# The last layer's first product by Strassen-Winograd on quarters, with weight sums made by accumulating DMAs

## The chip, the cores and the metric

One core of a Trainium2 chip runs the whole program. The metric is the device time of one execution in microseconds (us), lower is better. Differences under about 0.3% cannot be told from none.

The core has five engines with a queue each, executed in order: PE (matrix products), DVE and ACT (elementwise work; ACT also applies a scale and a bias in one instruction), POOL (elementwise work and DMAs) and SP (here it only issues DMAs). A product accumulates in PSUM, of which the program uses four buffers of two banks. Everything else lies in SBUF (128 partitions) or in device memory (HBM).

## The reference

```python
def _A_ref(x, w_r, w_i):                      # x: 2048 x 640
    return irfft2(rfft2(x) * (w_r + 1j * w_i))

def _B_ref(x, w1, b1, w2, b2):                # mixes along the 2048 rows
    h = _layernorm(x)
    u = gelu(einsum("bsd,sf->bdf", h, w1) + b1)        # F = 1728
    y = einsum("bdf,fs->bds", u, w2) + b2
    return y.transpose(0, 2, 1)

x = x + _A_ref(_layernorm(x), A_w_r, A_w_i)
x = x + _B_ref(_layernorm(x), B_w1, B_b1, B_w2, B_b2)
x = x + _A_ref(_layernorm(x), A_w_r, A_w_i)
x = x + _B_ref(_layernorm(x), B_w1, B_b1, B_w2, B_b2)
```

Both B layers use the same w1 and w2. All of it is float32, and the result must agree to float32 accuracy.

## The kernel before

The four layers run one after the other: A (`a1`, `a2`), B (`b1st`), A (`a1`, `a2`), B (`b2nd`). The change concerns the last one, `b2nd`, and one thing in `b1st`.

To multiply float32 numbers with float16 products, each operand is split in a high and a low float16 part: ACT writes `hi = scale * x`, DVE writes `lo = scale * x - hi`, and `mm3` adds three products, hi times hi, hi times lo and lo times hi. The names `wh`, `wl`, `hh`, `hl`, `u` and `wo` are such parts.

`h`, the normalised input, has 16 row blocks j of 128 x 640, each stored as two halves of 320. `w1` has 14 column tiles of 128 (the last has 64 columns twice, once for the high and once for the low product), `w2` 16 column tiles over 14 row blocks.

First product of `b2nd`: `SEQ` orders the 14 tiles in pairs (t, t + 7). A tile's two raw halves of 128 x 1024 float32 (512 KB) are loaded on SP four tiles ahead (`ahead`, `wload`), split by `wsplit` one tile ahead, and multiplied by 16 blocks of h: 16 x 2 halves x 3 = 96 matmuls, 64 for the last tile. Then come scale, bias and gelu, and `usplit` splits the result u into the parts that the second product needs: with t and t + 7 and the two halves of 320 u is a 2 x 2 matrix of quarters, and the parts are those quarters and their sums T1 to T4.

The second product is already done by Strassen-Winograd: with A a pair of w2 tiles (d, d + 8) cut in quarters A11, A12, A21, A22, and S1 = A21 + A22, S2 = S1 - A11, S3 = A11 - A21, S4 = A12 - S2, seven products of quarters replace eight. For each d `form` makes an S on DVE, `hi` (ACT) and `lo` (DVE) split all seven left operands, `product` runs 7 x 3 = 21 matmuls, and `evict` combines the result into `xt`, the residual with the bias added by `xbias` on ACT. The last u block to be ready, `LATE`, is left out of products 2 and 3 at first and added after them.

The order of work: within one engine the instructions run in program order where `pin` is set, and elsewhere in the order that the framework's scheduler chose at build time. Waits between engines are semaphores; a DMA on SP's or POOL's queue waits in that queue, and what stands behind it waits too. Up to eight DMAs of SP are under way at a time. A product needs a PSUM buffer, which is free once the product four back (with `big`, in turn) has been evicted.

## Time and profile before

| what | value |
|---|---|
| median of three runs | 1030.15 us (1028.54, 1030.15, 1031.58) |
| the profiled execution | 1028.95 us |
| its span, first to last instruction | 1027.2 us |
| mean granted TensorE clock | 0.980 |
| last layer (`b2nd`), first matmul to end | 684.76 to 1027.2 us |
| first product of it | 684.76 to 863.73 us |
| second product of it | 863.73 to 1023.7 us |

The span is that of the profiled execution; 1.75 us of its time lie outside it. In rows that group instructions, "xN" is their number, then follow busy us and mean ns of one, then the idle time of the engine before them and what released it. A timeline row begins with start and duration in us; rows of the chain of waits do so too, and name engine and output.

### The profile page before, as it was taken

What the parts mean: (1) busy time and instruction counts of PE and PEld (TensorE: products, weight loads), DVE (VectorE), ACT (ScalarE), POOL (GpSimd) and SP (SyncE); (2) the same over time, 40 slices, a digit from 0 to 9 for tenths busy, and PEclk for the clock granted to TensorE, in tenths of its full rate; (3) what the DMA queues carried; (4) which work ended last, traced back from release to release, by engine and by line L of the source; (5) the groups of instructions that cost most, each with busy time, mean ns of one, the idle gap of its engine ahead of it and who ended that gap; (6) DMA issues with size and microseconds to landing.
All of it is one profiled execution on the core that took longest, in us unless ns stands there. A gap on an engine that the chain in (4) does not pass through costs nothing.

```text
span 1027.2 us, 20943 instructions
## 1 busy us (share of the span) xinstructions
PE 986.3 (96%) x8379; PEld 735.7 (72%) x8379; DVE 725.5 (71%) x1422; ACT 571.2 (56%) x874; POOL 265.7 (26%) x438
## 2 busy tenths in 40 slices
PE   4889999999999999999998999999999999999998
PEld 3768777677777777777776787776777777777776
DVE  7968978954333956666666797897655564988885
ACT  5847768675554556555542575774544454544541
POOL 6927857500000002222222675780000000000000
PEclk9589999999999999999999999999999999999999
DMA  7855356522222264444312644756322232445511
GB/s 230 277 173 168 116 167 222 207 83 99 77 77 74 72 233 155 138 135 123 124 55 86 214 125 130 223 177 210 108 82 83 72 109 77 141 154 175 164 44 52
DMA packets 55738, 139.48 MB, mean 136 GB/s; under 512 B 6461, under 2 KB 12249, under 8 KB 55641
## 3 DMA queue, kind: packets, MB, share of 16 engines
q1 hardware_dynamic: 54200, 131.97, 40.1%
q0 software_dynamic: 1440, 6.17, 2.0%
q8 instruction: 66, 1.08, 0.4%
q14 instruction: 32, 0.25, 0.1%
HBM read 115.05 MB, written 23.07 MB: 134 GB/s over the span
## 4 chain that ended last, share of the span: by engine, by line
PE 76%; DVE 13%; POOL 3%; issue 3%; DMA 2%; ACT 2%; SPq 0%; POOLq 0%; DVEq 0%; ACTq 0%
PE ps L59 76%; DVE st L59 2%; POOL xt L59 2%; DVE xt L59 2%; DVE f L59 1%; DVE Yl L59 1%; DVE s1l L59 1%; DVE hl L59 1%; DVE ta L59 1%; ACT eh L59 1%; DVE el L59 1%; DMA rest<-s1l 1%; POOL r L59 1%; DVE tb L59 1%; DMA stk<-rest 1%
## 5 line engine op out<-in xcount | busy, mean ns | idle before, releaser
L59 PEld LDWEIGHTS <-wh 128*128 128x128 f16 x2992 | 289.7, 98 | 113.4 <-issue 1.8
L59 PEld LDWEIGHTS <-wl 128*128 128x128 f16 x1616 | 157.9, 98 | 62.2 <-DVE wl L59 0.9
L59 PE MATMUL ps<-hh,wh 128*128 128x320 f16 x896 | 186.6, 299 | 0.7 <-ACT hh L59 0.7
L59 PE MATMUL ps<-hl,wh 128*128 128x320 f16 x896 | 184.7, 299 | 0.0
L59 PE MATMUL ps<-hh,wl 128*128 128x320 f16 x832 | 171.4, 299 | 0.6 <-DVE wl L59 0.6
L59 DVE SCALAR_TENSOR_TENSOR wl<-raw,s,wh 128x1024 f16<-128x1024 f32 (+2 forms) x88 | 105.4, 1202 | 87.4 <-ACT wh L59 87.3
L59 PE MATMUL ps<-uh,wl 128*128 128x320 f16 x448 | 133.1, 299 | 0.0
L59 PE MATMUL ps<-ul,wh 128*128 128x320 f16 x448 | 133.1, 299 | 0.0
L59 ACT ACTIVATE wh<-raw,s 128x1024 f16<-128x1024 f32 (+2 forms) x92 | 94.7, 1047 | 68.4 <-PE ps L59 61.6
L59 PE MATMUL ps<-uh,wh 128*128 128x320 f16 x416 | 124.3, 299 | 0.0
L59 ACT ACTIVATE junk<-raw 128x896 bf16<-128x896 f32 (+1 forms) x60 | 59.6, 994 | 46.5 <-DMA raw<-w 46.4
L59 POOL TENSOR_TENSOR r<-v,mh 128x1 f32<-128x1 f32 x64 | 37.4, 584 | 132.2 <-DVE nm L59 122.6
L59 PE MATMUL ps<-tDi,Yh 128*128 128x322 f16 x320 | 71.3, 300 | 0.2
L59 PE MATMUL ps<-u,wo 128*128 128x320 f16 x504 | 69.9, 299 | 0.0
L59 DVE TENSOR_TENSOR f<-eo 128x256 f32<-128x256 f32 (+1 forms) x124 | 39.1, 368 | 38.8 <-POOL eo L59 38.1
L59 PEld LDWEIGHTS <-wo 128*128 128x128 f16 x504 | 49.3, 98 | 19.1
L59 POOL TENSOR_TENSOR xt<-xt,ec 128x320 f32<-128x320 f32 x64 | 52.4, 841 | 32.8 <-DVE xt L59 32.6
L59 PE MATMUL ps<-ph,tS 128*128 128x321 f16 (+2 forms) x288 | 59.6, 289 | 1.3 <-DVE tb L59 1.3
L59 ACT ACTIVATE z<-xt,nb,r 128x640 f32<-128x640 f32 x31 | 28.5, 919 | 55.8 <-POOL z L59 43.5
L59 DVE BATCH_NORM_STATS2 st<-xt 128x6 f32<-128x320 f32 x126 | 55.3, 481 | 5.7 <-DMA xt<-x 4.6
L59 PE MATMUL ps<-tM,f 128*128 128x128 f32 x160 | 39.5, 426 | 19.8 <-DVE f L59 19.8
L59 POOL TENSOR_TENSOR eo<-z 128x320 f32<-128x320 f32 x62 | 53.3, 880 | 17.1 <-ACT z L59 15.1
(174 smaller groups left out, 1877.0 us busy)
## 6 DMA issues: line engine op xcount, KB each, us to landing
raw<-w SPq DMA_DIRECT2D x56, 512.0 KB
xt<-x SPq DMA_DIRECT2D x79, 320.0 KB
w<-w SPq DMA_DIRECT2D x48, 321.0 KB
x<-xt SPq DMA_DIRECT2D x47, 320.0 KB
raw<-w SPq DMA_DIRECT2D x32, 448.0 KB
raw<-w2z SPq DMA_DIRECT2D x32, 448.0 KB
out<-xt SPq DMA_DIRECT2D x15, 320.0 KB
tIM<-tIM POOLq DMA_DIRECT2D x8, 512.0 KB, 5.6
```

What stands on the lines that cost most here:

```text
L59: i = f(*a, **k)
```

## The change

1. In `b1st`, after a tile's split, `wstore` writes its high and low parts to HBM: those of w1 (`wst`, on POOL's queue) and those of w2 (`wst2`, on SP's). Of the tiles t and t + 7 (or d + 8) it keeps A11, A12 and A22; A21 is never multiplied alone. Tiles 6 and 13 of w1 are not stored.
2. In `b2nd`, tiles 6 and 13 of w1 are multiplied as before (96 + 64 matmuls). The other twelve form six pairs (d, d + 7), d = 0 to 5, and each pair takes seven products of quarters of 8 x 3 = 24 matmuls, 168 in place of 192. A11, A12 and A22 are read back split (`fetch`, on SP, four products ahead). S1 to S4 are made in SBUF by DMAs on POOL's queue that add to what is there (`more`, `accum_op=ADD`): a base is loaded on SP (`begin`), and each `more` adds a quarter of w1 from HBM. Signs are moved to the other operand and the eviction, so only sums are needed: S1 = A21 + A22, S2 = S1 + A11, S4 = S2 + A12 and S3 = A11 + A21. For pair 0 each S has its own buffer and its adds are issued at the start of the layer; for the others S1, S2 and S4 are one buffer in turn, and the next add is issued after the low part of the one before. `hi` and `lo` are now for S only.
3. The right operands are sums of quarters of h, made in place on DVE (`tsum`, 128 x 4 x 320 each) and split by `thi` (ACT) and `tlo` (DVE). The parts of h are made four blocks at a time (`hlow`).
4. Each product is evicted by itself (`evict`: A11 twice on ACT, S1 twice on ACT, S2 and S3 two steps on DVE, and so on). The order of products interleaves pairs 0 to 2 and 4, 5 (`first`, `end`).
5. In the second product A11, A12 and A22 come from `wst2` (with a `memset` on POOL of the half of the last row block that is padding), S1 to S4 are formed and split as before. The raw parts of w2 (`load2`), not loaded ahead during the first product, are issued after the fetches for its first six products. The pairs 0 and 1 are interleaved, and the first four products leave `LATE` out at first.

```diff
-SEQ = [t + 7 * i for t in (0, 6, 1, 2, 3, 4, 5) for i in range(2)]
+SEQ = [6, 13]
...
+        self.wst = {
+            t: self.dram.tile([128, 2, 2, 8, 128] if t < 6 else [128, 2, 8, 128], F16, name=f"wst{t}")
+            for t in range(NFT - 1) if t != 6
+        }
+        self.wst2 = {
+            t: self.dram.tile([128, 2, 2, 7, 128] if t < NQ else [128, 2, 7, 128], F16, name=f"wstb{t}") for t in range(NJ)
+        }
...
+        k, t, n = self.wtile(m)
+        st, whole, eng = (self.wst2, NQ, self.nc.sync) if k else (self.wst, 6, self.nc.gpsimd)
+        if t not in st:
+            return
+        for i, w in enumerate(self.w[m]):
+            q = w[:, :n].rearrange("p (c b) f -> p c b f", c=2)
+            eng.dma_start(*((st[t][:, :, i], q) if t < whole else (st[t][:, i], q[:, 1])))
...
                 self.wsplit(m + 1, (c,))
+                if c:
+                    self.wstore(m + 1)
...
+        for j in range(8, NJ):
+            T.activation(hhb[:, j - 8], hf[j], AF.Copy)
...
+        PB = {"A11": "B11", "S1": "T1", "S2": "T2", "A12": "B21", "S3": "T3", "S4": "B22", "A22": "T4"}
...
+        first = "A11.0 A12.0 A11.1 A12.1 S1.0 S2.0 S3.0 S4.0 A22.0 S1.1 S1.2 A11.2 S2.1 S3.1 A22.1 S4.1 A12.2 S2.2 S3.2 A22.2 S4.2"
+        end = "S1.4 A11.4 A12.4 S2.4 S3.4 S1.5 A22.4 S4.4 A11.5 S2.5 A12.5 S3.5 S4.5 A22.5"
+        one = first.split() + each([3], "S1 A11 A12 S2 S3 A22 S4") + end.split()
+        two = "A11.0 A11.1 A12.0 A12.1 A22.0 A22.1 S1.0 S2.0 S3.0 S4.0 S1.1 S2.1 S3.1 S4.1".split()
+        two += each(range(2, NQ), "A11 S1 S2 S3 A12 S4 A22")
+        N1, NP = len(one), len(one) + len(two)
+        ops = [(int(q[-1]), q[:-2], PB[q[:-2]]) for q in one + two]
+        at = {ops[n][:2]: n for n in range(N1)}
...
+        places = [(px, "wo0"), (px, "wo1"), (self.wp[0], "wl"), (self.wp[1], "wl"), (self.wp[0], "wh"), (self.wp[1], "wh")]
...
+        def begin(d, a):
+            pool, tag = (self.wr[1], "Sa") if a == "S1" else (self.wr[0], "raw")
+            cur[d, a] = raw(pool, tag, 2, 8)
+            nc.sync.dma_start(cur[d, a], w1(d, "A21" if a == "S1" else "A11"))
+
+        def more(d, a, b):
+            G.dma_start(cur[d, a], w1(d, b), accum_op=ADD)
...
+        def fetch(n):
+            if n >= NP or ops[n][1][0] == "S":
+                return
+            f, (d, a, _) = int(n < N1), ops[n]
+            st, m = (self.wst, d) if f else (self.wst2, d)
+            w = place(n, 8 if f else 7)
+            nc.sync.dma_start(w, st[m][:, int(a[2]) - 1] if a[1] == "1" else st[m + (7 if f else NQ)])
+            if not f and a[2] == "2":
+                G.memset(w[64:, :, 6], 0.0)
...
+            if n < N1:
+                src[n] = cur[d, a] if (d, a) in cur else cur[d, "S1"]
+            w = place(n, 8 if n < N1 else 7)
+            T.activation(w[:, 0], src[n], AF.Identity, scale=scale(n))
...
+            V.scalar_tensor_tensor(w[:, 1], src[n], scale(n), w[:, 0], op0=MUL, op1=SUB)
+            if d and n < N1 and a in ("S1", "S2"):
+                more(d, "S1", "A11" if a == "S1" else "A12")
...
+        def tsum(a, c, W=V):
+            j, k = slice(4 * c, 4 * c + 4), slice(8 + 4 * c, 12 + 4 * c)
+            B11, B12, B21, B22 = hfa[:, j, 0], hfa[:, j, 1], hfa[:, k, 0], hfa[:, k, 1]
+            o, x, y = {"T1": (B12, B12, B11), "T2": (B22, B22, B12), "T3": (B11, B22, B11), "T4": (B21, B21, B22)}[a]
+            W.tensor_tensor(o, x, y, op=SUB)
...
+        def thi(a):
...
+                T.activation(TT[a][0][:, 4 * c:4 * c + 4], tsrc(a, c), AF.Copy)
...
+            for c in range(2):
+                j = slice(4 * c, 4 * c + 4)
+                V.tensor_tensor(TT[a][1][:, j], tsrc(a, c), TT[a][0][:, j], op=SUB)
...
+        def hlow(c):
+            j = slice(4 * c % 8, 4 * c % 8 + 4)
+            if c < 2:
...
+            else:
+                V.tensor_tensor(hlb[:, j], hfa[:, 4 * c:4 * c + 4], hhb[:, j], op=SUB)
...
+            if a == "A11":
+                ms[d] = self.t(p, [128, 320], F32, "m", 2)
+                act(ms[d])
+                act(f[:, 0], bias=b0)
+            if a == "A12":
+                add(f[:, 0], f[:, 0])
+            if a == "S1":
+                act(f[:, 1], k=self.c1n[:, d:d + 1], bias=b0)
+                act(f[:, 3], bias=b1)
+            if a == "S2":
+                vs[d] = self.t(p, [128, 320], F32, "v", 1)
+                add(vs[d], ms[d], SUB)
+                V.tensor_tensor(f[:, 1], f[:, 1], vs[d], op=SUB)
+            if a == "S3":
+                add(vs[d], vs[d], SUB)
+                T.activation(f[:, 2], vs[d], AF.Identity, scale=-1.0, bias=b1)
+                V.tensor_tensor(f[:, 3], f[:, 3], vs[d], op=SUB)
+            if a == "S4":
+                add(f[:, 1], f[:, 1])
+            if a == "A22":
+                add(f[:, 2], f[:, 2])
...
+        for d in range(1, ND):
+            n, k = at[d, "S1"], at[d, "S3"]
+            stage[max(n - 9, 0)].append(lam(begin, d, "S1"))
+            stage[max(n - 8, 0)].append(lam(more, d, "S1", "A22"))
+            stage[max(k - 11, 0)].append(lam(begin, d, "S3"))
+            stage[max(k - 10, 0)].append(lam(more, d, "S3", "A21"))
...
+        fetch(0)
+        fetch(1)
+        begin(0, "S1")
+        more(0, "S1", "A22")
+        self.wsplit(1, hi=False)
+        begin(0, "S3")
+        pr = self.push("br", side=self.sp)
+        for a in ("S2", "S4"):
+            cur[0, a] = pr.tile([128, 8, 128], F32, name=f"{a}r{self.n}")
+            nc.sync.dma_start(cur[0, a], w1(0, "A21"))
+        for a, q in (("S2", "A22"), ("S4", "A22"), ("S2", "A11"), ("S3", "A21"), ("S4", "A11"), ("S4", "A12")):
+            more(0, a, q)
+        for e in stage[0]:
+            e()
...
+        early, late, low, high = range(NJ - 4), range(NJ - 4, NJ), range(8), range(8, NJ)
+        for js in (early, late):
+            prod(pss[0], wh0, hhigh, js, start=True)
+            prod(pss[0], wl0, hhigh, js)
+            prod(pss[1], wh1, hhigh, js, start=True)
+        fetch(2)
+        fetch(3)
+        hlow(0)
+        hlow(1)
+        for i, w in enumerate((wh0, wh1)):
+            prod(pss[i], w, hlows, low)
+        product(0)
+        hlow(2)
+        hlow(3)
+        for i, w in enumerate((wh0, wh1)):
+            prod(pss[i], w, hlows, high, stop=True)
+        for a in ("T1", "T2"):
+            for c in range(2):
+                tsum(a, c)
+        thi("T1")
+        hi(4)
+        thi("T2")
+        tlo("T1")
+        lo(4)
+        hi(5)
+        tlo("T2")
...
+        T.activation(f[:, A2], pv, AF.Identity, scale=cc, bias=bb)
+        pv, sw = pss[1][:, :, :320], f[:, A4]
+        T.activation(sw[:64], pv[64:], AF.Copy)
+        T.activation(sw[64:], pv[:64], AF.Copy)
+        V.tensor_tensor(sw, pv, sw, op=ADD)
...
+        lo(5)
+        thi("T3")
+        hi(6)
+        tlo("T3")
+        lo(6)
+        last[2] += [lam(tsum, "T4", 0), lam(tsum, "T4", 1), lam(thi, "T4")]
+        last[3] += [lam(tlo, "T4")]
+        last[6] += [dup1, g0(0), g1(0), g0(1), g0(2), g1(1), g1(2), g0(3)]
...
+        for n in range(1, N1):
+            product(n)
+            for e in first[n]:
+                e()
+            if n == 1:
+                hi(7)
+            if n == 2:
+                lo(7)
+            if n > 4:
+                hi(n + 3)
+                lo(n + 3)
+            for e in last[n]:
+                e()
+            for e in stage[n]:
+                e()
+            fetch(n + 4)
...
+        evict(D5, "A22")
...
+        left = {d: 7 for d in range(NQ)}
+        for (d, a), n in at2.items():
+            if a[0] == "S":
+                n -= N1
+                todo[n - 4 - (d > 1 and a == "S1")].append(lam(form, N1 + n, p))
+        for d in range(2):
+            for a in ("A21", "A22", "A11", "A12"):
+                load2(d, a)
+            xload(d)
+        xload(2)
         xbias(0)
-        FORM = {3: 5, 5: 4, 6: 4, 1: 4}
-        for n in range(NP + 1):
...
+        xbias(1)
+        rest = [j for j in range(7) if j != LATE]
+        for n in range(NP2 + 1):
+            if n < NP2:
+                d, a, _ = ops[N1 + n]
+                if n > 3 or n % 2 == 0:
+                    big = self.big()
+                bank[n] = big[:, n % 2 if n < 4 else 0, :320]
+                product(n, rest if n < 4 else rest + [LATE], stop=n > 3)
             if n == 3:
-                for k in (2, 3):
-                    product(k, [LATE])
-            for k in {0: (), 3: (), 4: (2, 3)}.get(n, (n - 1,)):
+                for k in range(4):
+                    product(k, [LATE], start=False)
+            for k in {0: (), 1: (), 2: (), 3: (), 4: (0, 1, 2, 3)}.get(n, (n - 1,)):
                 evict(k)
...
+            if n == 5:
+                xbias(2)
+            if n > 2:
+                hi(N1 + n + 3)
+            if n > 3:
+                lo(N1 + n + 2)
+            for e in todo[n]:
+                e()
+            fetch(N1 + n + 4)
+            for e in extra[n]:
+                e()
+            if n < NP2 and a == "S4" and d + 2 < NQ:
+                for b in ("A21", "A22", "A11", "A12"):
+                    load2(d + 2, b)
```

How instructions move, at the two places of which the prediction speaks. First the start of the last layer on ACT; `hf` is h in float32, `T1h` the high part of T1, `wh <- Sa` and `wh <- S2r` the high parts of S1.0 and S2.0 (pair 0), `fr` tiles 6 and 13, `m` and `f` the eviction of A11.0, `wo <- raw` and `wo <- S4r` the high parts of S3.0 and S4.0. Before, the splits of the next tiles of w1 stood there:

```order
L59 ACTIVATE hh_1371_10059<-hf_1202_9237 128x640
L59 ACTIVATE hh_1371_10061<-hf_1202_9238 128x640
L59 ACTIVATE wl_10366<-raw_10129,s_72 128x8x64
L59 ACTIVATE f_10303<-ps_10141,b1s,c_74 128x640
L59 ACTIVATE q_10305<-ps_10141,b1s,c_74 128x640
L59 ACTIVATE wh_10311<-raw_10125,s_72 128x1024
```

Now:

```order
L59 ACTIVATE T1h_10117<-hf_9285 128x1280 x2
L59 ACTIVATE wh_10362<-Sa_10137,sp_79 128x1024
L59 ACTIVATE T2h_10119<-hf_9285 128x1280 x2
L59 ACTIVATE wh_10369<-S2r_10147,sp_79 128x1024
L59 ACTIVATE fr_10377<-ps_10159,b1s,c_74 128x640
L59 ACTIVATE fr_10377<-ps_10160 64x640 x2
L59 ACTIVATE T3h_10121<-hf_9285 128x1280 x2
L59 ACTIVATE wo_1391_10387<-raw_10142,sp_79 128x1024
L59 ACTIVATE m_10418<-ps_10297,c_74 128x320
L59 ACTIVATE f_10417<-ps_10297,b1s,c_74 128x320
L59 ACTIVATE wo_1395_10421<-S4r_10149,sp_79 128x1024
L59 ACTIVATE T4h_10123<-hf_9285 128x1280 x2
```

Between the end of h and the first eviction of a product there are now four operand sums' high parts and three of S. On DVE, which feeds them, stands at the same place now:

```order
L59 TENSOR_TENSOR hf_9285<-hf_9285 128x4x320 x4
L59 TENSOR_TENSOR T1l_10118<-hf_9285,T1h_10117 128x1280 x2
L59 SCALAR_TENSOR_TENSOR wh_10362<-Sa_10137,sp_79,wh_10362 128x1024
L59 TENSOR_TENSOR T2l_10120<-hf_9285,T2h_10119 128x1280 x2
L59 TENSOR_TENSOR fr_10377<-ps_10160,fr_10377 128x640
L59 TENSOR_TENSOR hf_9285<-hf_9285 128x4x320 x2
L59 SCALAR_TENSOR_TENSOR wh_10369<-S2r_10147,sp_79,wh_10369 128x1024
L59 TENSOR_TENSOR T3l_10122<-hf_9285,T3h_10121 128x1280 x2
L59 SCALAR_TENSOR_TENSOR wo_1391_10387<-raw_10142,sp_79,wo_1391_10387 128x1024
L59 SCALAR_TENSOR_TENSOR f_10417<-ps_10392,c_74,f_10417 128x320
L59 SCALAR_TENSOR_TENSOR wo_1395_10421<-S4r_10149,sp_79,wo_1395_10421 128x1024
L59 TENSOR_TENSOR hf_9285<-hf_9285 128x4x320 x2
```

The rows `hf <- hf` are the sums T1 and T2 (four rows), T3 and T4 (two each), and the last `f` row is the eviction of A12.0.

The second place is the boundary of the two products on SP. Before, the raw parts of w2 came in among those of w1, four tiles ahead, and the `xt` of the residual after them:

```order
L834 DMA raw_11177<-w 128x1024
L834 DMA raw_11179<-w 128x1024
L834 DMA raw_11295<-w2z 128x896
L834 DMA raw_11297<-w2z 128x896
L834 DMA raw_11417<-w2z 128x896
L834 DMA raw_11419<-w2z 128x896
```

Now (`wstb` are the stored parts of w2; the second of these rows is A22.1's fetch, into the place of the first product's last operand):

```order
L1201 DMA wh_11872<-wstb_102 128x1792
L1201 DMA wh_11893<-wstb_103 128x1792
L1404 DMA raw_11824<-w2z 128x896
L1404 DMA raw_11826<-w2z 128x896
L1404 DMA raw_11828<-w2z 128x896
L1404 DMA raw_11830<-w2z 128x896
L1559 DMA xt_11832<-x_0_146 128x640
L1559 DMA xt_11832<-x_8_154 128x640
L1404 DMA raw_11835<-w2z 128x896
L1404 DMA raw_11837<-w2z 128x896
L1404 DMA raw_11839<-w2z 128x896
L1404 DMA raw_11841<-w2z 128x896
```

The second pair's two `xt` rows follow. On ACT there stands now, after the last high part of u:

```order
L59 ACTIVATE u_1427_10804<-q_11756,su 128x320
L59 ACTIVATE xt_11832<-xt_11832,b2s 128x640 x2
L59 ACTIVATE xt_11843<-xt_11843,b2s 128x640 x2
L59 ACTIVATE wo_1531_11947<-S_1530_11915,sp 128x896
L59 ACTIVATE m_1534_11973<-ps_11853,c_75 128x320
L59 ACTIVATE m_1535_11976<-ps_11853,c_75 128x320
L59 ACTIVATE wo_1536_11981<-S_1532_11949,sp 128x896
```

The bias rows of the pairs 0 and 1 stand ahead of the first high part of an S (S1.0), and the evictions `m` of A11.0 and A11.1 behind it.

More of the change, by code (lines that the diff above doesn't have):

```diff
@@ L1139, in b2nd @@
-        px = self.push("px", side=self.sp)
-        pu = self.push("u", side=self.sp)
-        u = [pu.tile([128, 2, 7, 320], F16, name=f"u{f}_{self.n}") for f in range(7)]
-        p = self.push("b1", side=self.sq)
-        for m in (2, 3, 4, 5):
-            self.wload(m)
-        def ahead(m):
-            self.wload(m + 4)
-            if m + 1 < NFT:
-                self.wopen(m + 1)
-        PQ = ("A11", "B11"), ("S1", "T1"), ("S2", "T2"), ("S3", "T3"), ("A12", "B21"), ("S4", "B22"), ("A22", "T4")
@@ L1166, in form @@
+        def form(n, p=None):
             if n >= NP:
@@ new lines, in b2nd, with product, gelu @@
+        bank = {}
+        def product(n):
+            d, a, b = ops[n]
+            o = bank[d, a] = self.big()[:, 0, :320]
+            w = wo[n]
+            for j in range(8):
+                self.mm3(o, (w[:, 0, j], w[:, 1, j]), operand(b, j), j == 0, j == 7)
+        gc, gs = 1.0 / GC, GS * GC
+        fs, qs = {}, {}
+        def gelu(k, x, q, s=slice(None)):
+            x, q = x[:, s], q[:, s]
+            if k == 0:
+                T.activation(q, x, AF.Square)
+            if k == 1:
+                V.scalar_tensor_tensor(q, q, gc, x, op0=ADD, op1=MUL)
+            if k == 2:
+                T.activation(q, q, AF.Tanh, scale=gs)
+            if k == 3:
+                V.scalar_tensor_tensor(x, q, 1.0, x, op0=ADD, op1=MUL)
@@ new lines, in b2nd, with half, go, split1 @@
+        u = {t0: self.u6}
+        for k in range(3):
+            last[9 + k].append(lambda k=k: usplit(k, t0, f))
+        last[12] = [uopen] + last[12]
+        D5 = ND - 1
+        q5 = {}
+        def half(i, *ks):
+            def go():
+                if i // 2 not in q5:
+                    q5[i // 2] = self.t(p, [128, 2, 320], F32, "q", 2)
+                for k in ks:
+                    gelu(k, fs[D5][:, i:i + 1], q5[i // 2][:, i % 2:i % 2 + 1])
+            return go
+        def split1(i, n, x):
+            return [lambda: uhi(D5, i, n, fs[D5][:, x:x + n]), lambda: ulo(D5, i, n, fs[D5][:, x:x + n])]
```

360 lines of the change are left out of this document (183 added, 177 removed).

## The prediction

> **What bounds the kernel now.** I read the page first, then the chain of waits, then windows and the timeline of the last layer.
>
> ```profile
> span 1027.2 us, 20943 instructions
> PE 986.3 (96%) x8379; PEld 735.7 (72%) x8379; DVE 725.5 (71%) x1422; ACT 571.2 (56%) x874; POOL 265.7 (26%) x438
> 703.39 3.96 DMA raw<-w
> 712.13 311.52 PE ps L59 x2292
> ```
>
> PE is busy for 96% of the span, and the last link but one of the chain is 311.52 us of matmuls with nothing between them. Whatever takes matmuls out of that stretch shortens the kernel, as long as nothing makes PE wait instead. The stretches of the last layer (start, first product, second product: columns are us, then busy us of PE, PEld, DVE, ACT, POOL, then clock, DMA share, GB/s):
>
> ```profile
> 684.75:700.00 15.25, 14.90 (x109) 10.41 (x108) 14.54 (x27) 7.62 (x12) 7.40 (x10) 1.00 0.35 115
> 700.00:863.70 163.70, 163.09 (x1201) 117.21 (x1200) 92.68 (x117) 79.19 (x97) 0.00 (x0) 1.00 0.34 107
> 863.70:1023.50 159.80, 159.80 (x1178) 114.92 (x1175) 131.28 (x162) 72.01 (x85) 0.00 (x0) 1.00 0.38 121
> ```
>
> In the first product DVE is at 57% and ACT at 48%; both can take more. The timeline gives the edges and the price of a matmul:
>
> ```profile
> 684.76 2.35 PE L59 MATMUL ps<-hh,wh 128*128 128x320 f16 x16
> 695.34 0.43 PE L59 MATMUL ps<-hh,wh 128*128 128x320 f16 x2 [0.19 <-ACT hh L59]
> 697.78 2.47 PE L59 MATMUL ps<-hh,wl 128*128 128x320 f16 x17
> 863.73 8.31 PE L59 MATMUL ps<-u,wo 128*128 128x320 f16 x60
> 1017.77 3.02 PE L59 MATMUL ps<-u,wh 128*128 128x320 f16 x21
> 1020.62 3.02 PE L59 MATMUL ps<-u,wl 128*128 128x320 f16 x21
> 1023.68 0.55 DVE xt L59
> ```
>
> From 1017.77 to 1020.62 are 21 matmuls: 2.85 us, 0.1357 us each. The first product (13 tiles of 96 and one of 64, 1312 matmuls) runs from 684.76 to 863.73, 178.97 us, which is 1312 x 0.1357 and 0.9 of waiting.
>
> **The gain.** The first product becomes 96 + 64 matmuls (tiles 6 and 13) and 6 pairs x 7 products x 24 = 1008: 1168, so 144 fewer. The second product keeps 56 x 21. 144 x 0.1357 = 19.5 us if PE never waits more than now. The end after 1023.68 is unchanged.
>
> **Work that hides.** In layer 1 about 9.4 MB of w1 parts and 11 MB of w2 parts are stored in some 180 and 215 us, about 52 GB/s each.
>
> ```profile
> 215.00:265.00 50.00, 50.00 (x374) 36.04 (x373) 21.47 (x52) 29.72 (x44) 0.00 (x0) 1.00 0.29 98
> 365.00:415.00 50.00, 50.00 (x392) 36.50 (x391) 28.79 (x79) 29.55 (x43) 8.68 (x21) 1.00 0.58 193
> 35.00:40.00 5.00, 4.54 (x19) 3.91 (x18) 4.96 (x14) 4.82 (x13) 4.57 (x10) 0.50 0.98 345
> ```
>
> There PE is busy throughout with the DMA engines at 0.29 to 0.58, and they have moved 345 GB/s when full, so the stores cost nothing; without that cover each 50 us would have 2.6 MB more, 7.5 us. In the steady part of the first product a pair takes 168 x 0.1357 = 22.8 us of PE. Its work for DVE and ACT comes from these rows:
>
> ```profile
> L59 DVE SCALAR_TENSOR_TENSOR wl<-raw,s,wh 128x1024 f16<-128x1024 f32 x24 | 30.7, 1284 | 44.4 <-ACT wh L59 44.4
> L59 ACT ACTIVATE wh<-raw,s 128x1024 f16<-128x1024 f32 x22 | 25.2, 1144 | 40.3 <-PE ps L59 35.0 <-issue 5.2
> L59 DVE SCALAR_TENSOR_TENSOR xt<-ps,cp,xt 128x320 f32<-128x320 f32 x32 | 17.6, 551 | 20.7 <-ACT m L59 11.7 <-PE ps L59 8.9
> L59 ACT ACTIVATE m<-ps,cp 128x320 f32<-128x320 f32 x8 | 4.2, 522 | 11.6 <-PE ps L59 11.6
> L59 DVE TENSOR_TENSOR fs<-f,fs 128x320 f32<-128x320 f32 x14 | 6.8, 489 | 0.2
> L59 DVE SCALAR_TENSOR_TENSOR u<-fs,su,u 128x960 f16<-128x960 f32 x6 | 7.3, 1218 | 1.8 <-ACT u L59 1.8
> L59 ACT ACTIVATE u<-fs,su 128x960 f16<-128x960 f32 x6 | 6.6, 1096 | 4.0 <-DVE fs L59 4.0
> L59 DVE TENSOR_TENSOR hl<-hf,hh 128x640 f16<-128x640 f32 x16 | 11.8, 820 | 0.0
> L59 ACT ACTIVATE hh<-hf 128x640 f16<-128x640 f32 x2 | 1.3, 722 | 0.0
> L59 DVE SCALAR_TENSOR_TENSOR u<-f,su,u 128x640 f16<-128x640 f32 x7 | 6.2, 880 | 0.0
> L59 ACT ACTIVATE u<-f,su 128x640 f16<-128x640 f32 x7 | 5.8, 827 | 8.2 <-DVE f L59 8.2
> ```
>
> DVE: four low parts of S (5.1), five evictions from PSUM (2.8), six sums of 320 (2.9), four gelu steps of 640 at the 0.82 of hl (3.3) and splits of u of 320, 640 and 1280 (3.0): 17 us, 75%. ACT: four high parts (4.6), six evictions of 320 (3.1), four gelu steps at the 0.72 of hh (2.9) and u's high parts (2.8): 13 us, 59%. Both fit, at shares that DVE has in the second product now (131.28 of 159.80) without a wait of PE. In the second product three splits of seven leave DVE and ACT; per 20 us three fetches of 0.459 MB come in addition, so the traffic rises from about 158 to 227 GB/s (4.5 MB in 20 us; the row is further down), under 345. I cost both at 0.
>
> **The start, +5.0 us.** Here the chain over DVE and ACT is longer than PE's work. Clocks, from the timeline:
>
> ```profile
> 689.83 2.47 DVE L59 SCALAR_TENSOR_TENSOR wl<-raw,s,wh 128x1024 f16<-128x1024 f32 x2
> 692.21 8.17 DVE L59 TENSOR_TENSOR hl<-hf,hh 128x640 f16<-128x640 f32 x11
> 691.61 1.48 POOL L59 TENSOR_SCALAR nb<-mv,r 128x1 f32<-128x1 f32 x1
> L59 DVE SCALAR_TENSOR_TENSOR wh<-raw,s,wl 128x512 f16<-128x512 f32 x2 | 1.5, 752 | 0.0
> L59 ACT ACTIVATE sw<-ps 64x640 f32<-64x640 f32 x2 | 1.4, 698 | 2.0 <-PE ps L59 2.0
> L59 DVE TENSOR_TENSOR sw<-ps,sw 128x640 f32<-128x640 f32 x1 | 0.8, 825 | 2.9 <-ACT sw L59 2.9
> ```
>
> No operation of 1280 is in the trace. On DVE 640 to 960 adds 1.056 ns an element (an estimate from u's rows, 880 and 1218), so 820 + 640 x 1.056 = 1.50, and 1.42 back to back (8.17 / 11 = 0.743 against 820). On ACT, by u's 827 and 1096 and hh's 722, likewise 1.26. DVE: tile 13's halves end at 691.3, the four low parts of h at 697.0, the two of 2560 at 702.6, the sums T1 and T2 at 708.2, T1's low parts at 711.1, low S1.0 at 712.3, T2's at 715.2, tile 13's fold at 716.0, sums T3 at 718.8, low S2.0 at 720.1, T3's at 722.9, low S3.0 at 724.2, A12.0's eviction at 724.7. ACT follows DVE: T3's high parts end at 720.1, high S3.0 at 721.2, and only then A11.0 is evicted, 722.3. PE: 96 high matmuls to 697.8 as now, 32 low to 702.1, A11.0 to 705.4, 32 to 709.7, A12.0 713.0, A11.1 716.4, A12.1 719.6. S1.0 needs A11.0's buffer: 722.3, a wait of 2.7; S2.0 runs to 728.8. S3.0 needs A11.1's, whose eviction stands on ACT behind high S4.0 and T4's high parts, which wait for T4's sums (728.8): 731.1, a wait of 2.3. After it DVE has caught up. Bounds: 2 (operations as short as their overlapped time everywhere) and 9 (0.15 us more for each of some 25 hand-overs).
>
> **The accumulating DMAs, 0 in the sum.** None is in the trace. The nearest rows are POOL's plain loads of the same size:
>
> ```profile
> L59 POOL DMA_DIRECT2D tIM<-tIM x6: 573/625/629, 131.9 to 660.8; - x6
> DMA to landing us min/median/max: 4.2/5.6/7.5
> ```
>
> POOL is free at 693.1. S2.0 needs two in a row and S4.0 three: by 7.5 each 708.1 and 715.6, while ACT reaches them at about 712 and 722. In a pair S1 to S2 to S4 has three products, 9.8 us, for a landing and a split (2.4), so up to 7.4 costs nothing, and PE feels it only some 3 us later. Per pair five plain transfers and four sums of 0.524 MB (128 x 1024 x 4 bytes): 13.7 us of full engines if a sum costs as much as a copy. With a factor k the time is (2.62 + 2.10 k) / 0.345, which passes 22.8 at k = 2.5. I take the row, so 0, and keep k up to 2.75 for the range.
>
> **Between the products, +7.0 us.** SP issues in order. Its last fetch ahead (A22.1 of w2) waits for the last matmul of the first product, t0; behind it stand four raw parts of w2, two xt, four raw, two xt. ACT adds the bias to both xt pairs before the high part of S1.0, and m1 of the first two products comes after that. Until the second xt pair: 9 x 0.459 + 4 x 0.328 = 5.44 MB, at 345 GB/s 15.8 us, and 2.4 us for landing (3.96 for a raw of 0.524 MB, in the chain, less 1.5): t0 + 18.2.
>
> ```profile
> L59 ACT ACTIVATE xt<-xt,b2s 128x640 f32<-128x640 f32 x16 | 12.3, 813 | 0.0
> L59 ACT ACTIVATE wo<-S,sp 128x896 f16<-128x896 f32 x16 | 16.7, 1041 | 39.2 <-DVE S L59 39.2
> L59 DVE SCALAR_TENSOR_TENSOR wo<-S,sp,wo 128x896 f16<-128x896 f32 x16 | 18.3, 1145 | 0.0
> 960.00:980.00 20.00, 20.00 (x149) 14.39 (x148) 16.79 (x21) 8.93 (x10) 0.00 (x0) 1.00 0.51 158
> ```
>
> Bias 0.8, high part 1.04 (20.0), m1, eviction, m1, eviction 2.15 (22.2), two evictions and the low part 2.25: t0 + 24.4. PE reaches S1.0 after six products, 126 x 0.1357 = 17.1, and its third matmul needs the low part: a wait of 7.0. The next products then come at DVE's pace, about 2.85 each, so nothing is won back. Before, these loads stand ahead of time. The ends are 4.6 (no landing time) and 8.3 (the 121 / 0.38 = 318 GB/s of the second product's row). [...]
>
> **The sum.** The profiled run was 1028.95 (span 1027.2 and 1.75 around it): 1028.95 - 19.5 + 5.0 + 7.0 = 1021.4. The three runs shown have median 1030.15, 1.2 above the profiled one; I take half of that: **1022**.
>
> **Rivals.** *Nearly the whole gain, 1010 to 1014*: ACT's bias waits and the start's buffers come free earlier than walked. For it: now PE waits 0.19 there and DVE is seldom the last. Against: the order of ACT and SP leaves no other way. 19.5 less 4 or so: 1028.95 - 15.5 = 1013. *The sums in DMA become the bound, 1031 to 1050*: from k = 2.5 each of five pairs waits. At k = 3 a pair takes 25.9, +3.1 x 5 = 15, and the seven sums of the start with 2.6 MB of plain loads (13.6 MB, 39 us) end at 732 where ACT wants 722: +10. 1021 + 25 = 1046. For it: 27 sums on one queue beside the fetches. Against: the engines have room for a factor of two. [...] *The gain is used up, 1027 to 1033*: DVE does not catch up after the start, and each later pair loses 1 us more to its order of waits: 1021.4 + 6 = 1027.
>
> **How the numbers follow.** Forecast (1014 to 1027) 0.47, nearly whole gain 0.18, sums in DMA 0.22, used up 0.13. Leaving out a third of the second and the part of the third above k = 2.75 (1036), the range is 1010 to 1036; the forecast's own is 1014 to 1027. A measurement here tells 0.3%, 3.1 us, from no change: faster (under 1027) 0.65, same 0.11, slower 0.24.
>
> **What would show it.** In the changed profile: 144 matmuls fewer; PE waiting on ACT f or m about 720 and 729, some 5 us together; ACT idle on DMA xt after the first product and PE waiting some 7 us there; no wait for ACT wh or wo behind DMA Sa in the steady pairs. Landing times of Sa over 8 us, or PE waits at every pair, would speak for the second rival. A PE busy through the boundary would break my largest loss.

## The result: 1036.5 us, slower by 0.6%

| kernel | median us | runs | ratio to before |
|---|---|---|---|
| before | 1030.24 | 6 | 1 |
| changed | 1036.48 (1033.50 to 1039.52) | 6 | 1.0064 [1.0040, 1.0087] |

The prediction was 1022, faster. The profiled run of the changed kernel took 1039.52, 3.0 above the median of its six, with a span of 1037.7. From its page: the span, PE's busy time and count, the chain by line, and POOL's DMA queue (packets, MB, share of the 16 engines' span).

```profile
span 1037.7 us, 20977 instructions
PE 974.2 (94%) x8235; PEld 724.2 (70%) x8235; DVE 737.6 (71%) x1446; ACT 560.4 (54%) x872; POOL 308.7 (30%) x505
q0 software_dynamic: 8016, 29.77, 12.0%
PE ps L59 68%; DMA S4r<-w 3%; DMA xt<-x 2%; POOL xt L59 2%; DVE st L59 2%; DVE f L59 2%; DVE Yl L59 1%; DVE xt L59 1%; DVE s1l L59 1%; DVE hl L59 1%; DVE ta L59 1%; ACT eh L59 1%; DMA raw<-w2z 1%; POOL eo L59 1%; POOL r L59 1%
```

The 144 matmuls are gone (8379 to 8235), and PE is busy 12.1 us less (not 19.5: part of its work ran at a lower clock, below), yet the span is 10.5 longer: PE waits instead. A DMA of `S4r`, a sum of the first pair, now stands in the chain. The timeline of PE before the last layer's products gives a mark that divides the loss: the last matmul of the second A layer's inverse transform (`tIM`). The first A layer has such a matmul too. Both, in the changed kernel, and then in the kernel before:

```profile
188.02 0.31 PE L59 MATMUL ps<-eh,tIM 128*128 128x322 f32 x1
...
696.72 0.31 PE L59 MATMUL ps<-eh,tIM 128*128 128x322 f32 x1
```

```profile
186.54 0.30 PE L59 MATMUL ps<-eh,tIM 128*128 128x322 f32 x1
...
684.61 0.31 PE L59 MATMUL ps<-eh,tIM 128*128 128x322 f32 x1
```

Up to this mark 12.1 us are lost, in a part of the program where little more was changed than that stores were added and `h` became one tile. Of them 1.5 are there already at the first layer's row, ahead of every store; over all profiles of this document that row lies between 184.8 and 188.0, in no order that an edit would give. So profiles are compared below from that row to the mark: 498.1 us before, 508.7 in the changed kernel, 10.6 more. From the mark to the end the old kernel takes 342.6 and the new 341.0, so of the 19.5 only 1.6 remain. Where the other 17.9 went, PE's waits from 680 on say (in total, times, longest):

```profile
PE ps L59 <- ACT f L59: 7.1, 2, 5.4
PE ps L59 <- DVE xt L59: 3.9, 1, 3.9
PE ps L59 <- ACT fr L59: 1.8, 1, 1.8
PE ps L59 <- DVE wo L59: 1.3, 1, 1.3
```

That is 8.9 at the start (`f`, `fr`) and 5.2 between the products (`xt`, `wo`). The waits of 5.4 and of 3.9 end at 747.5 and 887.6. Windows of 2 us behind them (columns as in the windows before; the clock stands third from the end):

```profile
746.00:748.00 2.00, 0.47 (x2) 0.26 (x2) 2.00 (x3) 2.00 (x5) 0.00 (x0) 0.79 1.05 281
748.00:750.00 2.00, 2.00 (x9) 1.19 (x8) 1.90 (x5) 2.00 (x3) 0.00 (x0) 0.50 0.52 156
750.00:752.00 2.00, 2.00 (x15) 1.32 (x14) 1.85 (x3) 1.74 (x4) 0.86 (x1) 0.86 0.00 0
...
890.00:892.00 2.00, 2.00 (x10) 1.12 (x8) 2.00 (x4) 1.04 (x1) 0.00 (x0) 0.50 0.28 41
892.00:894.00 2.00, 2.00 (x9) 1.14 (x8) 2.00 (x4) 0.85 (x1) 0.00 (x0) 0.52 0.91 349
```

The granted clock is halved for some 3 us behind the first gap and some 6 behind the second, which the wait of 1.3 (`wo`) interrupts. By PE's timeline the 24 matmuls of S3.0, the product behind the first gap, take 4.73 us from start to start (747.53 to 752.26) where 24 x 0.1357 = 3.26 would do: 1.5 lost. Behind the second, 40 take 7.57 (889.56 to 897.13) where 5.43 would do: 2.1. Waits of 14.1 and clock of 3.6, less the 0.9 of waits that the old kernel has behind its mark, make 16.8 of the 17.9; 1.1 is not attributed.

For the loss ahead of the mark, SP's timeline in layer 1's second product (start, us, queue, line):

```profile
353.63 8.92 SPq L853 DMA_DIRECT2D raw<-w  x3
363.51 0.60 SPq L891 DMA_DIRECT2D wstb<-wh  x1
364.78 0.51 SPq L891 DMA_DIRECT2D wstb<-wl  x1
365.34 0.84 SPq L853 DMA_DIRECT2D raw<-w  x1
```

The load of a `raw` part (w2, line 853) now comes right behind a pair of stores (`wstb`, line 891), which wait for the finished parts. SP takes them in order, so a load leaves only when the tile before it has been split and stored. Window 380 to 400 shows the price, first before, then changed:

```profile
380.00:400.00 20.00, 20.00 (x159) 14.64 (x158) 9.84 (x33) 11.35 (x16) 4.61 (x11) 1.00 0.67 235
```

```profile
380.00:400.00 20.00, 15.51 (x110) 10.77 (x110) 8.33 (x24) 9.21 (x13) 3.54 (x9) 0.98 0.89 313
```

PE is no longer full, and the DMA engines are at 0.89 and 313 GB/s where the prediction had seen room.

### The profile page after: what moved, and what is told of

It is laid out like the page before. It is cut to its first block, busy times and chain, and to the rows that moved or that the text cites. A ratio compares the mean times of both kernels' runs of the same rounds, so it can differ in the third digit from the quotient of the medians.

```text
span 1037.7 us, 20977 instructions
## 1 busy us (share of the span) xinstructions
PE 974.2 (94%) x8235; PEld 724.2 (70%) x8235; DVE 737.6 (71%) x1446; ACT 560.4 (54%) x872; POOL 308.7 (30%) x505
## 4 chain that ended last, share of the span: by engine, by line
PE 68%; DVE 13%; DMA 6%; POOL 4%; ACT 4%; issue 3%; SPq 0%; POOLq 0%; DVEq 0%; ACTq 0%
PE ps L59 68%; DMA S4r<-w 3%; DMA xt<-x 2%; POOL xt L59 2%; DVE st L59 2%; DVE f L59 2%; DVE Yl L59 1%; DVE xt L59 1%; DVE s1l L59 1%; DVE hl L59 1%; DVE ta L59 1%; ACT eh L59 1%; DMA raw<-w2z 1%; POOL eo L59 1%; POOL r L59 1%
## 5 line engine op out<-in xcount | busy, mean ns | idle before, releaser
L59 PEld LDWEIGHTS <-wh 128*128 128x128 f16 x2602 | 252.0, 98 | 105.3 <-issue 6.7
L59 PEld LDWEIGHTS <-wo 128*128 128x128 f16 x756 | 75.4, 100 | 42.3 <-issue 7.7
L59 PE MATMUL ps<-hl,wh 128*128 128x320 f16 x504 | 104.1, 299 | 0.0
L59 DVE SCALAR_TENSOR_TENSOR wl<-raw,s,wh 128x896 f16<-128x896 f32 (+2 forms) x64 | 74.6, 1170 | 25.1 <-ACT wh L59 25.1
L59 ACT ACTIVATE wh<-raw,s 128x896 f16<-128x896 f32 (+2 forms) x68 | 67.3, 1011 | 10.7 <-PE ps L59 9.1
L59 PE MATMUL ps<-u,wo 128*128 128x320 f16 x420 | 61.4, 306 | 5.2 <-DVE xt L59 3.9
L59 PE MATMUL ps<-hha,wh 128*128 128x320 f16 x304 | 61.5, 299 | 1.1 <-ACT wh L59 1.1
L59 PE MATMUL ps<-tM,f 128*128 128x128 f32 x160 | 37.6, 402 | 22.5 <-DMA xt<-x 12.4
L59 PE MATMUL ps<-tDi,Yl 128*128 128x322 f16 x192 | 55.7, 299 | 1.7 <-DVE Yl L59 1.7
```

Of the source, the lines that this page charges most:

```text
L59: i = f(*a, **k)
```

## The experiments

Times are medians, and the runs of before beside them had medians of 1029.35 (first four kernels), 1029.81 (next four) and 1028.80 (last four); ratios are to these.

**1. The stores, put into the kernel before.** `before_stores` is the kernel before with `wstore` and its calls; `before_w1stores` keeps only w1's, which POOL issues.

```diff
+        self.wstore(0)
+        self.wstore(1)
...
+                if c:
+                    self.wstore(m + 1)
```

> The kernel before plus the change's stores of the split w1 and w2 parts in layer 1, which nobody reads. In the changed kernel's profile the last layer starts 12 us later than before. If the stores cost that (theory 1: SP's queue stands still behind the w2 stores; theory 2: their traffic), 1039 to 1042 us against 1030.2. If the shift comes from the other edits (theory 3), 1030 to 1032.

> The kernel before plus only the w1 stores, on POOL's queue. Theory 1 (waiting stores in SP's queue): 1030 to 1032. Theory 2 (traffic, 9.4 of the 20.4 MB): 1034 to 1037. Theory 3: 1030 to 1031.

Measured: 1036.90, ratio 1.0069 [1.0050, 1.0089], and 1029.82, 1.0008 [0.9997, 1.0019]. The stores of w1 cost nothing that can be told; those of w2 on SP cost 7. PE's waits in layer 1 of `before_stores` that are not in the kernel before:

```profile
PE ps L59 <- DVE sqb L59: 3.5, 1, 3.5
PE ps L59 <- DVE ul L59: 1.5, 1, 1.5
```

`sqb` is the scale's sum over a raw part: the load was late.

**2. The changed kernel without most stores, and with later ones.** `after_nostores` stores tile 0 alone and fetches it in place of every other (the A parts of both products are then others than the reference's). `after_late` keeps all, but issues a w2 tile's stores on SP one tile later, behind the next `raw` load.

```diff
-                if c:
+                if c and m + 1 < NFT:
                     self.wstore(m + 1)
+                elif c:
+                    held.append((m + 1, self.w[m + 1]))
```

> The changed kernel with the stores of tile 0 alone (4 in place of 56); every fetch of the last layer reads that tile, so the first and second product use wrong A parts, with the same bytes moved there. Theories 1 and 2: the 12 us at the start of the last layer go, 1024 to 1027 us. Theory 3: 1035 to 1037.

> The changed kernel with each w2 store issued one tile later on SP, behind the next loads, when its split is long done. Theory 1 (the queue stands still): 1026 to 1031. Theory 2 (traffic): 1035 to 1038, unchanged.

Measured: 1032.21, 1.0025 [1.0010, 1.0040], and 1033.75, 1.0036 [1.0019, 1.0053]. In the changed kernel the stores cost some 4 us (1.0064 to 1.0025); issued later they cost about 1, which the intervals do not tell from nothing. Single runs of `after_late` lie between 1028.9 and 1036.0, and its profiled one, 1030.02, is the second fastest of ten; why they spread so was not found. From the first layer's row to the mark `after_nostores` takes 502.2 us and `after_late` 501.9, so the stall is gone in both, but even without stores it is 4.1 more than before. `after_late` moves the same bytes as the changed kernel, so the stall is one of the queue and not of the traffic; the medians point the same way, but their intervals overlap. ACT's timeline at the start of layer 1's products in `after_nostores` shows one cause:

```profile
209.14 1.06 ACT L59 ACTIVATE junk<-raw 128x1024 bf16<-128x1024 f32 x1 [10.58 <-DMA raw<-w]
```

The scan of a raw w1 part waits 10.58 us for its load. Its buffer reuses the memory of `h`, and since `h` is one tile, the load waits for the last reader of all of it. Experiment 7 undoes this.

**3. SP's order between the products.** `late_xt` is `after_late` with the first two `xt` pairs ahead of most raw parts of w2.

```diff
-        for d in range(2):
-            for a in ("A21", "A22", "A11", "A12"):
-                load2(d, a)
-            xload(d)
+        load2(0, "A21")
+        load2(0, "A22")
+        xload(0)
+        xload(1)
+        load2(0, "A11")
+        load2(0, "A12")
+        for a in ("A21", "A22", "A11", "A12"):
+            load2(1, a)
         xload(2)
```

> The changed kernel with late w2 stores, and at the boundary of the two products SP issues two raw parts, both xt pairs, then the other raw parts. If the wait there is for the second xt pair, as the prediction says, the 4.8 us of waits and some 3 us of half clock after them go: 1025 to 1028 against 1033.8 without it. If the next thing (raw parts, DVE) takes its place: 1031 to 1034.

Measured: 1026.25, 0.9961 [0.9945, 0.9977], 0.75% or 7.7 us better than its base and faster than before. The windows at the boundary, first `after_late`, then `late_xt`:

```profile
860.00:880.00 20.00, 15.17 (x110) 10.45 (x109) 10.54 (x18) 10.53 (x16) 0.31 (x1) 0.95 0.77 302
880.00:900.00 20.00, 20.00 (x132) 13.66 (x131) 19.90 (x25) 7.30 (x7) 0.00 (x0) 0.88 0.69 226
```

```profile
860.00:880.00 20.00, 18.39 (x134) 12.79 (x133) 15.08 (x24) 12.20 (x19) 0.31 (x1) 1.00 0.84 321
880.00:900.00 20.00, 20.00 (x149) 14.26 (x148) 19.86 (x26) 7.29 (x7) 0.00 (x0) 1.00 0.73 235
```

In 40 us 283 matmuls start where 242 did: 41 x 0.1357 = 5.6 us, part of it by the clock, which stays at 1.00. The two profiled runs differ by 5.9 us behind the mark (340.3 and 334.4).

**4. ACT's order at the start.** `late_evict` is `after_late` with A11.0 evicted before T3's high parts and A11.1 before T4's.

```diff
         V.tensor_tensor(sw, pv, sw, op=ADD)
+        evict(0, "A11")
...
+            if n == 2:
+                evict(1, "A11")
             for e in last[n]:
                 e()
```

> The changed kernel with late w2 stores, and ACT evicts A11.0 before T3's high parts and A11.1 before T4's. Theory A (the prediction's: the chain over DVE and ACT makes the waits at the start): they fall from 8.3 to about 2, 1027 to 1030. Theory B (S4.0's accumulating DMAs make them): 1033 to 1035.

Measured: 1033.41, 1.0030 [1.0015, 1.0045], no different from its base. ACT's timeline:

```profile
730.08 1.15 ACT L59 ACTIVATE wo<-S4r,sp 128x1024 f16<-128x1024 f32 x1 [4.84 <-issue]
```

ACT stands still 4.84 us before the high part of S4.0, whose sum has not landed, and the eviction of A11.1 is queued behind it. Of PE's two waits for `f`, 6.8 us in the base, one is gone; the other, 4.4, stays behind the late sum. What the order gains there is lost further on: in the 40 us from 100 us after the mark PE's windows count 282 matmuls, 300 in the base, and PE now waits for low parts of S (`wh` 0.6, `wl` 0.4).

**5. The first pair's sums on POOL instead of in the DMAs.** `late_pool` loads the four quarters of pair 0 plainly and makes S1.0 to S4.0 with five additions on POOL.

```diff
+        for a, b in (("A22", "A21"), ("A21", "A11"), ("A12", "A11"), ("A11", "A22"), ("A12", "A22")):
+            G.tensor_tensor(raw0[a], raw0[a], raw0[b], op=ADD)
```

> The changed kernel with late w2 stores, and the four sums of pair 0 made by five additions on POOL from four plain loads, in place of seven accumulating DMAs on four loads. Theory A: 1032 to 1034, the start's waits stay near 5. Theory B: the start's waits fall to about 5 or less and the clock stays up, 1026 to 1030.

Measured: 1038.55, 1.0083 [1.0067, 1.0100], the slowest of all; from the mark to the end the profile has 347.3 us for the 340.3 of its base. DVE is slower while POOL adds, 10.01 and 9.87 us for two groups that take 5.69 and 5.55 on DVE in `late_xt`, where POOL adds nothing. POOL's timeline, then DVE's:

```profile
702.54 3.48 POOL L59 TENSOR_TENSOR Sa<-Sa,raw 128x1024 f32<-128x1024 f32 x1
714.43 4.93 POOL L59 TENSOR_TENSOR A12r<-A12r,A22r 128x1024 f32<-128x1024 f32 x1
```

```profile
697.36 10.01 DVE L59 TENSOR_TENSOR hl<-hf,hha 128x1280 f16<-128x1280 f32 x4
707.29 9.87 DVE L59 TENSOR_TENSOR hlb<-hf,hhb 128x2560 f16<-128x2560 f32 x2
```

Once POOL is done (719.36) DVE is back at its pace: of T1's two sums (717.08 to 722.12) the first lets ACT start at 720.75, so the second takes some 1.4 us, as in `late_xt`, where T1's and T2's four take 5.69. What POOL's additions would take by themselves no run shows.

**6. All three together, and `h` in separate tiles in layer 1.** `late_all` joins 3, 4 and 5 and splits `hf` again where the layer is the first.

```diff
+        if first:
+            self.hf = [ph.tile([128, 2, 320], F32, name=f"hf{j}_{self.n}") for j in range(NJ)]
+        else:
+            self.hfa = ph.tile([128, NJ, 2, 320], F32, name=f"hf{self.n}")
```

> All three of these at once, and in layer 1 the normalised input in 16 tiles as before (in the changed kernel it is one tile, and the raw loads that reuse its place wait for its last reader). If the waits are separate: 1012 to 1019. If taking one away brings up another: 1024 to 1031.

Measured: 1030.62, 1.0009 [0.9996, 1.0022]: what the order and the tiles give is about what the additions on POOL cost by themselves in experiment 5 (4.8 us above their base).

**7. Separate tiles alone.** `xt_sep` is `late_xt` with the edit of 6.

> late_xt with h of the first layer in sixteen separate tiles again (the last layer keeps its one tile). Theory: in one tile the raw loads that reuse its memory wait for the last reader of all of it, which costs layer 1 about 2 us: last tIM matmul about 686.5 instead of 688.5, time 1024 (0.994 to 0.995 of before). Rival (that wait is hidden behind PE's other work): last tIM matmul within 0.5 of late_xt's, time 1026.

Measured: 1023.61, 0.9947 [0.9932, 0.9961], 0.14% better than `late_xt`, which is less than can be told, and the intervals overlap. The mark is at 687.8 for 688.5, but the first layer ended 1.6 later in this profile; from its row to the mark it is 500.3 us for 502.6, 2.3 less, where about 2 were expected. The scan that waits 10.58 us above and 9.01 in `late_xt` has short waits here, the longest:

```profile
201.40 1.06 ACT L59 ACTIVATE junk<-raw 128x1024 bf16<-128x1024 f32 x1 [2.17 <-DMA raw<-w]
```

The wait is shown to come from the one tile; its price, 1.4 us by the medians and 2.3 by the profiles, is at the edge of what these runs tell.

**8. Plain copies in place of the sums.** `xt_copy` is `late_xt` with `accum_op` left out, so the S matrices of the first product are single quarters of w1.

```diff
-            G.dma_start(cur[d, a], w1(d, b), accum_op=ADD)
+            G.dma_start(cur[d, a], w1(d, b))
```

> late_xt with every accumulating DMA turned into a plain copy of the same bytes on the same queue; the matrices S1 to S4 of the first product are then single quarters of w1, so its products are others. Theory (a sum costs 1.5 to 2 copies): POOL queue's share of the engines falls from 12.1% to about 8%, median landing of Sa's and S4r's from 7.4 and 8.9 to 5 and 6 us, S4.0's high part at the start 2 to 4 us earlier, time 1022 to 1025. Rival (a sum costs as much as a copy, and what is late is the number of them): share, landings and time as late_xt, 1026.

Measured: 1017.55, 0.9882 [0.9864, 0.9900], 0.79% or 8.1 us below `late_xt`. POOL's queue and the span in `before_w1stores` (without these DMAs), in `xt_copy` and in `late_xt`:

```profile
span 1027.5 us, 21002 instructions
q0 software_dynamic: 4128, 15.61, 4.4%
```

```profile
span 1017.0 us, 20974 instructions
q0 software_dynamic: 8016, 29.77, 8.5%
```

```profile
span 1022.9 us, 20974 instructions
q0 software_dynamic: 8016, 29.77, 12.1%
```

The 27 DMAs move 14.16 MB. As copies they take 86.4 - 45.2 = 41.2 us of the sixteen engines, which is 344 GB/s; as sums 123.8 - 45.2 = 78.6. A sum costs 1.91 copies. The landing of S4.0's sums, `late_xt` and then `xt_copy`:

```profile
DMA to landing us min/median/max: 7.8/8.9/15.5
```

```profile
DMA to landing us min/median/max: 5.2/6.7/11.9
```

In `xt_copy` S4.0's high part starts right behind A11.0's eviction, and PE's waits for `f` fall from 6.3 (longest 4.7) to 3.7 (longest 1.9). The wait for `fr`, 1.6, is gone, and the clock is not lowered any more, which makes the gain larger than expected. In `late_xt` it had been, behind the wait of 4.66:

```profile
740.00:742.00 2.00, 2.00 (x10) 1.14 (x9) 1.85 (x3) 2.00 (x4) 0.02 (x1) 0.58 0.03 12
```

There the 24 matmuls of S3.0 take 4.86 us (738.36 to 743.22) where 3.26 would do. So of the 7.5 us by which the profiles differ behind the mark (334.4 and 326.9) 4.2 are waits at the start and 1.6 clock; the rest lies at the boundary of the products, where `late_xt` has waits of 1.7 (`wo`, `u`) and `xt_copy` 0.2.

**9. The first pair's sums begun in the stage before.** `xt_early` is `xt_sep` with the bases of S2.0 and S4.0 loaded, and five of the sums issued, inside the loop of the inverse transform.

```diff
+        adds = {4: ("S2", "A22"), 5: ("S4", "A22"), 7: ("S2", "A11"), 8: ("S4", "A11"), 11: ("S4", "A12")}
...
+            if not first and i in adds:
+                a, q = adds[i]
+                G.dma_start(self.sr[a], w1(q), accum_op=ALU.add)
```

> xt_sep with the loads of S2.0's and S4.0's bases and five of the seven first accumulating DMAs issued one by one inside the loop before (the last layer's tIM stage), so that only S1.0's and S3.0's sums remain at the start. Theory (the first wave of seven sums is too late for S4.0): S4.0's high part starts on ACT right behind A11.0's eviction, about 727 instead of 731, PE's waits on ACT f fall from 6.3 to 3 to 4, time 1021 to 1023. Rival (the walk over DVE and ACT alone sets the start): the waits stay at 6, time 1024 as xt_sep. Second rival (adds disturb the loop that they are put into): last tIM matmul later by 1 to 3 us, time 1025 to 1027.

Measured: 1023.84, 0.9947 [0.9932, 0.9962], the same as `xt_sep`. ACT's timeline has no wait before S4.0 any more, and PE's longest wait for `f` is 1.94, behind which the clock stays at 1.00:

```profile
726.49 1.14 ACT L59 ACTIVATE wo<-S4r,sp 128x1024 f16<-128x1024 f32 x1
```

Behind the mark it is 2.6 us faster than `xt_sep` (331.2 for 333.8). But from the first layer's row to the mark it takes 503.6 us, 3.3 more, as the second rival had it: PE's waits for `el` and `eh` there grow from 1.6 to 3.4. Both halves of the expectation came true and cancel.

**10. With ACT's order of 4 on top.**

> xt_early, and on ACT A11.0 is evicted before T3's high parts and A11.1 before T4's (the order of late_evict, which gained 0.3 by itself behind the late sum). Theory (the late sum masked what the order is worth): PE's waits on ACT f fall under 1.5 us and the clock stays at 1.00 at 720 to 760, time 1018 to 1020. Rival (order worth nothing): as xt_early. Against before: faster by 0.9 to 1.2%.

Measured: 1020.95, 0.9923 [0.9910, 0.9936], faster than before by 0.8%. The order that was worth nothing behind a late sum is worth 2.5 us (0.9947 to 0.9923) when the sum is there, though the intervals still touch. Behind the mark the profiles differ by 1.4 (331.2 and 329.8): the waits for `f` fall from 3.7 to 0.7, and those for `wl` grow from 0.4 to 1.7. PE's windows in it:

```profile
720.00:740.00 20.00, 19.29 (x143) 13.77 (x142) 19.83 (x20) 13.67 (x16) 2.27 (x3) 1.00 0.58 139
...
760.00:780.00 20.00, 18.94 (x139) 13.22 (x138) 13.33 (x21) 9.76 (x12) 2.60 (x3) 1.00 0.83 197
```

The changed kernel has PE at 16.54 in 720 to 740. From 760 on small waits appear in the steady pairs, which neither it nor `xt_copy` has there (PE 20.00 in 760 to 780). ACT's timeline has it idle before two of S's high parts in these pairs, once by name for the sum's DMA:

```profile
775.53 1.15 ACT L59 ACTIVATE wl<-Sa,sp 128x1024 f16<-128x1024 f32 x1 [6.83 <-issue]
...
789.65 1.15 ACT L59 ACTIVATE wo<-Sa,sp 128x1024 f16<-128x1024 f32 x1 [3.93 <-DMA Sa<-w]
```

With the start shortened, the sums of the later pairs are late too.

## Why the prediction was wrong

**"The gain" was right.** 144 matmuls are gone, and in `xt_copy`, where most of the waits are gone too, the span from the mark (690.1) to the end is 326.9 against 342.6: 15.7 of the 19.5, the rest being 3.9 of waits.

**"Work that hides: the stores cost nothing" failed.** The argument was about bytes per second, and for w1's stores, on POOL, it held. For w2's the queue decides: they were put between SP's loads and wait for the parts to be made, so each load is held back (experiments 1 and 2). The price is 4 us in the changed kernel and 7 in the old, by the medians. The one tile for `h`, which the prediction did not cost at all, adds 1.4 to 2.3.

**"The accumulating DMAs, 0 in the sum" failed, and is the largest miss.** The price of a sum was taken from the plain loads' landing of at most 7.5 us, as if each had the engines to itself: S4.0's three in a row were put 22.5 us after POOL's last `nb`, which ends at 704.80 in the changed kernel. POOL's timeline there has all three, the window its DMA share, and ACT's timeline the high parts of S2.0 and S4.0:

```profile
706.22 1.54 POOL L59 DMA_DIRECT2D S4r<-w  x1
719.33 0.85 POOL L59 DMA_DIRECT2D S2r<-w  x1 [11.57 <-DMA S2r<-w]
...
722.26 0.85 POOL L59 DMA_DIRECT2D S4r<-w  x1 [1.20 <-DMA S4r<-w]
732.78 0.86 POOL L59 DMA_DIRECT2D S4r<-w  x1 [9.66 <-DMA S4r<-w]
```

```profile
700.00:720.00 20.00, 20.00 (x150) 14.41 (x148) 19.41 (x19) 7.13 (x10) 7.38 (x10) 1.00 0.95 256
```

```profile
725.11 1.15 ACT L59 ACTIVATE wh<-S2r,sp 128x1024 f16<-128x1024 f32 x1 [1.74 <-DMA S2r<-w]
...
739.98 1.15 ACT L59 ACTIVATE wo<-S4r,sp 128x1024 f16<-128x1024 f32 x1 [4.58 <-issue]
```

The three are issued at 706.22, 722.26 and 732.78, and ACT starts on S4.0 at 739.98: 35.2 us after `nb` in place of 22.5. Each is issued when the one before has landed, and the landings, 15.8, 10.0 and 7.1, add up; the first ran beside two other sums and the loads and fetches of the start, with the engines at 0.95. ACT had come to S4.0 at 735.4, as walked (722 + 12.1 = 734), and the eviction for which PE waits is queued behind it, so the wait that was put at 2.3 is 5.4. S2.0's two sums are late as well: ACT waits 1.74 for them just before `fr`, and PE 1.8 for `fr`; in `xt_copy` neither wait is there. The rival did add up the burst of the start, by its bytes alone: at k = 1.91 that sum gives 9.6 MB, 28 us from POOL's 693.1, so 721, in time for ACT. What it leaves out is that the sums wait for one another. The limit k = 2.5 was one for the steady pairs. There the step held at the measured 1.91, as a link of the changed kernel's chain of waits shows (start, us):

```profile
747.53 119.01 PE ps L59 x864
```

PE runs without a break from S3.0 through the five steady pairs. It does so behind a start that is late already: in `late_evict`, `xt_early` and `xt_early_evict`, where the start is shorter, these pairs have waits, and the median landing of `Sa`, 6.2 us in the changed kernel, is 7.6 and 7.5 in the last two, above the 7.4 that were to cost nothing. Turning the sums into copies is worth 8.1 us, some 6 of them at the start by experiment 8.

**"The start, +5.0" was right in its walk.** T1's low parts were put to end 26.5 us after the mark and end 26.1 after it (722.8). PE waits 1.7 for A11.0's eviction, where the walk had 2.7. In `xt_copy`, without the late sums, this wait is 1.8 and that for A11.1's is 1.9, where the walk had 2.3: 3.7 in all for 5.0. The order of evictions, which the walk named as the cause, takes the waits for `f` from 3.7 to 0.7 in experiment 10. The term was a little high; the late sums were not in it.

**"Between the products, +7.0" had the right cause, and its size partly by luck.** ACT's timeline in the changed kernel has the wait that was named, for the second `xt` pair, ahead of the bias:

```profile
882.90 1.55 ACT L59 ACTIVATE xt<-xt,b2s 128x640 f32<-128x640 f32 x2 [4.33 <-DMA xt<-x]
```

The pair is there 16.4 us after the last matmul of the first product (747.53 + 119.01 = 866.54) where 18.2 were forecast, and PE's waits are 5.2 in place of 7.0. The clock, which was not in the sum, adds 2.1. Experiment 3 takes 7.7 away by the medians.

**The clock** is not in the sum: the old kernel's last layer has it at 1.00 in every row of the prediction. In the runs PE's gaps of 3.15 (`xt_sep`), 3.94 and 5.40 (the changed kernel) and 4.66 us (`late_xt`) were followed by a clock of 0.50 to 0.68 in the next full window of 2 us, and `xt_early`'s gap of 1.94 by 1.00. In the changed kernel the matmuls behind the gap of 5.40 lost 1.5 us by it and those behind the gap of 3.94, with the wait of 1.29 that follows, 2.1. From what length on a gap lowers the clock was not measured.

Taken together: 1030.2 - 19.5, + 4 for stores, + 1.4 for the one tile, + 8.1 for sums, + 7.7 at the boundary and + 3.7 left at the start give 1035.6, against 1036.5. Most of these steps are differences between medians along one row of kernels, so that they add up shows little by itself. What they leave to test is `xt_copy`. At 0.9882 of 1030.2, or 1018.0, it lies 7.3 above the 1010.7 that the gain alone would give, and 3.7 at the start, 1.4 for the tile and some 1 for the late stores explain about 6 of that. The rival of the sums in DMA (1031 to 1050) has the measured time in it, in part by luck. Its part at the start came true in kind (+10 at k = 3; some 6 measured at 1.91), its slower pairs did not in the changed kernel, and the rest of the way to 1036 is made up by stores that no rival named.

## What to carry to other kernels

A transfer that is hidden by bandwidth can still cost its queue, as w2's stores did on SP (7 us in the old kernel): before adding a store, see which loads stand behind it and what it waits for. A DMA's price is that of the moment at which it is issued (in the changed kernel sums of one size landed after 5.4 to 15.8 us), so a burst at the start of a stage is summed up by itself, whatever the average share says, and not by its bytes alone: S4.0's three, each of which waits for the one before, added up their landings (15.8, 10.0 and 7.1). And an order on one engine can look worthless because something else is late: try it again once that is gone, and look again at what seemed free behind the delay.

## What the runs showed of the hardware

The same 27 DMAs took 1.91 times the engine time as sums (`late_xt`) that they took as copies (`xt_copy`): 78.6 us for 41.2, 14.16 MB. While POOL ran its additions of 128 x 1024 (3.5 to 4.9 us each, `late_pool`), DVE's two low parts of 128 x 2560 took 9.87 us, without them 5.55 (`late_xt`).
